# The last chunk's q, k and output turned by DMA, and a plan made anew, in a fused linear-attention and feed-forward kernel

## The chip, the cores and the metric

The kernel runs on one core of a Trainium2 chip. The metric is the device time of one execution in microseconds (us). A core has five engines with queues of their own: TensorE (PE in the profile; its weight loads are PEld), VectorE (DVE), ScalarE (ACT), GpSimd (POOL) and SyncE (SP, which here issues all DMAs). Each engine takes its instructions strictly in order, and waits on semaphores for what the others make.

## The reference

Two layers, one after the other. The first is a gated linear attention: for 4 batches and 8 heads, over 768 positions with a head size of 48, a 48 x 48 state decays by a gate f and takes up the outer product of k and v; the output is q times the state. The second layer takes the result as 3072 tokens of 384 features, through w_in (384 x 2048), the function h cos(h), and w_out (2048 x 384).

```python
f = 1.0 / (1.0 + np.exp(-f_logit))
for t in range(S):
    state = f[:, :, t, :, None] * state + np.einsum('bhd,bhe->bhde', k[:, :, t], v[:, :, t])
    y[:, :, t] = np.einsum('bhd,bhde->bhe', q[:, :, t], state)
...
x = attn_out.transpose(0, 2, 1, 3).reshape(B * S, H * D)
h = x @ w_in
return (h * np.cos(h)) @ w_out
```

## The kernel before

**Chunks.** The 768 positions of a batch are cut into 6 chunks of 128, so there are 24 chunks, numbered 0 to 23. `decay` (line 515) makes the running decay of two chunks at a time: the load of f_logit, Exp and Ln on ACT, a cumulative sum as matmuls on PE (op "cum"), and two Exp on ACT that give `b` and `bi` (line 578). Chunks 0 to 11 go in interleaved pairs through `attend2` (line 633), chunks 12 to 23 singly through `attend` (line 795).

**One chunk in `attend`.** POOL multiplies q by `b` and k by `bi` into the bf16 tile `qk` (op "qk", line 800). `qk` has to be turned, so that the head features lie on partitions. There are two ways. Either PE makes eight transposes into PSUM (op "tr", line 818) and DVE or ACT copies them out (op "qkt"); or, for chunks in `TURN_QK`, SP issues one DMA transpose from `qk` to the tile `qkt` (op "tq", line 809). Then PE makes the scores (line 831), DVE masks them into `am` (line 835), PE updates the state (op "ps", line 845; DVE and POOL scale it, lines 596 and 603), and PE makes y from the state and from `am` (lines 859 and 863). `finish` (line 612) copies y to the bf16 tile `yb` and turns it into a part of `xT`, again in one of two ways: three PE transposes (op "trx", line 626) and a copy (op "xe"), or, for chunks in `TURN_Y`, one DMA transpose from `yb` to `xT` (op "ty", line 618). All the plain copies of these helpers carry line 513.

**Units.** `moe` (line 894) takes two units of 128 tokens (chunks 0 and 1) and eleven of 256 (two chunks each). For a unit of 256, PE makes h in four blocks of 12 matmuls (line 907), ACT takes the cosine (line 915), DVE multiplies into `gT` (line 924), and PE makes the output, 16 matmuls for each chunk (line 934). It is copied to `ot`, and SP stores it (line 942). The first h of a unit waits for the whole `xT` of its chunks. The weights come in four pieces of w_in and four of w_out: a DMA each (line 479) into a staging tile, and a cast to bf16 on POOL, DVE or ACT (op "wc", line 485).

**Buffers that matter here.** `qk` four, `qkt` three, `ld` fourteen halves, `yb` two, `ot` four, the staging tiles and `gT` together six; of PSUM, three pairs of banks for h.

**The order.** It is not the order of the code. Every operation is first recorded by `Plan.op` (line 132) with its inputs, its outputs, a cost for each engine that could run it, and a priority. `Plan.run` (line 161) then lays out the whole program: it picks again and again, among the operations that could start within 120 ns of the earliest, the one of lowest priority number, gives it to the engine on which it would end first, and at last sorts everything by the planned start. So the program is a static order for each engine, PE's and SP's too. The numbers that steer it are tables:

- `PR` has a priority for each kind of operation and chunk, unit, group or piece: "f", "k", "q", "v" for the loads, "at" for the work of a chunk, "tq" and "ty" for the DMA transposes, "h" and "o" for the units, "w_in" and "w_out" for the loads of the weights, "wc" for their casts.
- `PR["gate"]` says, for each of the six groups of four chunks, after which cosine its first exponential may come. ACT has one function table for Exp and Ln and another for the cosine and loads a table at each change.
- `PIN` ties operations, by their number in the record, to one engine. Numbers 1, 3, 5 and 7 are the casts of the w_in pieces 0 to 3, and 9, 11, 13 and 15 those of w_out.
- `BLOCK`, `LEAD` and `FETCH` belong to `fetched` (line 167), which counts PE's instructions: a block of 256 is asked for when the one before it is entered, and if it is entered less than `FETCH` ns after it was asked for, the planned cost of that operation grows by the rest. With `FETCH` at 0 it never grows.
- In the first 36 us the plan also fills idle time of PE with matmuls on zeros (`keep_warm`, line 443, shown as line 448).

Of the kernel before, what the change touches and what calls it, by code (L numbers as in the profile page):

```python
# [116 lines left out]
class Plan:  # L117
# [4 lines left out]
    FORM = 96.0  # L122
    WARM = 1000.0, 36000.0
    SPARE = 300.0
    BLOCK, LEAD, FETCH = 256, 187, 0.0
    TABLE = 1290.0
    WINDOW = 120.0

# [3 lines left out]
    def op(self, name, eng, fn, reads=(), writes=(), prio=0.0, table=None, lat=0.0, grp=None,  # L132
           dma=None, form=("full", "full"), count=0):
        o = Op()
        if PIN.get(len(self.ops)) in eng:
            eng = {PIN[len(self.ops)]: eng[PIN[len(self.ops)]]}
        o.name, o.eng, o.fn, o.prio, o.table = name, eng, fn, prio, table
# [149 lines left out]
def apart(tc, o, base):  # L287
# [13 lines left out]
    if banks and len(others) == len(banks):  # L301
        for b in banks:
# [7 lines left out]
FREE_GROUPS = 1  # L310
HALVED = [0, 2]
COLUMNS = [0]
TURN_Y = range(14, 23)
TURN_QK = range(10, 23)
PR = {
    "at": [-27.91, -77.01, -56.28, -9.17, -0.94, -73.7, -81.2, 39.48, -37.57, -208.65, -211.06, -60.08,
          -83.16, -243.89, -50.42, -56.25, 1.3, -2.3, 29.67, 79.95, 98.34, -55.29, 97.21, 135.16],
    "dec": [17.99, -244.81, 110.38, -107.76, -115.06, -57.64],
    "f": [-126.5, 9.16, -68.42, 63.89, -29.77, -28.09, -25.9, -101.11, -12.97, -46.6, -13.01, -73.8, 5.03,
          -19.04, 46.31, -11.98, 36.02, -5.88, 14.64, -12.03, -9.82, 91.12, 135.61, 80.29],  # L320
    "h": [71.32, -87, -76.49, -17.17, 21.33, -10.88, 23.01, -55.39, -81.13, -168.15, 42.49, -185.2, -65.32],
    "k": [-86.38, -44.94, -46.44, -77.89, -10.71, -14.47, -10.3, 16.65, 19.58, 33.88, 24.75, -42.47, 93.38,
          56.3, 64.2, 82, 99.55, 66.33, 75.6, 103.33, 149.48, 152.06, 180.76, 236.21],
    "o": [-48.11, -58.72, 67.27, 96.81, 129.67, 114.46, -1.43, 88.44, -1.17, 210.3, 20.96, 63.38, 132.01],
    "q": [-102.19, 18.13, -43.75, -58.53, -20.96, -20.69, 3.65, 30.77, 13.57, 38.94, 22.63, -27.69, 43.05,
          64.32, 73.74, 93.93, 83.65, 126.33, 120.02, 148.55, 160.95, 173.59, 319.64, 340.67],
    "tq": [48.59, 92.1, 81.02, -144.86, -187.26, -106.78, -170.82, 10.27, -66.65, -84.42, -111.64, -134.39,
          -84.57, 73.12, -78.38, -82.54, -126.4, -224.07, -57.89, 90.43, 53.23, 51.1, 158.93, 99.76],
    "ty": [88.78, 44.77, 51.02, -49.47, -165.27, -158.37, -101.69, 50.45, 31.53, -89.25, 92.4, -10.66,
          -109.03, 30.59, -136.55, -158.16, -176.89, -143.38, -109.75, -9.6, -42.19, -39.15, -87.93, -26.78],  # L330
    "v": [-46.79, 17.23, -41.07, 7.71, -23.55, -71.11, 10.76, 43.67, 2.59, -102.67, 11.36, 155.56, 68.43,
          17.25, 83.31, 55.29, 17.8, 46.36, 78.93, 34.36, 62.06, 117.69, 104.33, 11.01],
    "w_in": [-39.88, -40.08, -39.64, -38.03],
    "w_out": [-34.2, -33.96, -37.04, -33.75],
    "wc": [-70.63, -33.41, 50, 25.03, -16.34, 18.34, -16.44, -221.86],
    "gate": [None, 2, 4, 12, 20, 24],
}
PIN = {1: "DVE", 7: "POOL", 9: "DVE", 11: "POOL", 13: "POOL", 15: "POOL", 34: "POOL", 35: "DVE", 36: "DVE", 37:
       "ACT", 39: "ACT", 43: "DVE", 55: "DVE", 82: "DVE", 101: "DVE", 103: "POOL", 104: "POOL", 105: "POOL",
       111: "ACT", 122: "ACT", 124: "DVE", 125: "DVE", 127: "ACT", 148: "DVE", 154: "ACT", 166: "DVE", 167:  # L340
       "DVE", 170: "ACT", 172: "ACT", 184: "ACT", 186: "ACT", 187: "DVE", 189: "ACT", 210: "ACT", 216: "ACT",
       228: "POOL", 229: "DVE", 230: "DVE", 231: "POOL", 232: "POOL", 234: "DVE", 238: "DVE", 248: "ACT", 250:
       "DVE", 251: "DVE", 274: "ACT", 280: "DVE", 292: "POOL", 294: "POOL", 295: "POOL", 296: "POOL", 302:
       "ACT", 315: "DVE", 316: "DVE", 318: "DVE", 357: "DVE", 360: "DVE", 361: "POOL", 373: "DVE", 399: "ACT",
       436: "POOL", 445: "ACT", 468: "DVE", 489: "ACT", 498: "DVE", 505: "POOL", 514: "DVE", 536: "DVE", 542:
       "ACT", 566: "ACT", 578: "DVE", 600: "ACT", 621: "ACT", 629: "ACT", 636: "POOL", 667: "DVE", 673: "ACT",
       688: "ACT", 697: "DVE", 704: "ACT", 735: "ACT", 741: "DVE", 756: "ACT", 765: "DVE", 774: "DVE", 778:
       "DVE", 801: "DVE", 813: "ACT"}


def build(nc, cpool, ppool, q, k, v, f_logit, moe_w_in, moe_w_out, out):
# [260 lines left out]
    def finish(n, y, ycut, prio):  # L612
# [3 lines left out]
             reads=[y], writes=[yb], prio=prio)  # L616
        if n in TURN_Y:
            P.op("ty", {"SP": 420.0}, lambda e: nc.sync.dma_start_transpose(out=x.ap, in_=yb.ap),
# [14 lines left out]
    def attend2(b, c, n, ld, bt, bi, prio):  # L633
# [6 lines left out]
        for i in range(2):  # L640
# [8 lines left out]
            reads=[vf], writes=[vb], prio=prio)  # L649
        turned = n in TURN_QK  # L650
        twin = lambda j, p, e: qkv()[:, j, e, 2 * p:2 * p + 2, :].rearrange("p h d -> p (h d)")
# [143 lines left out]
    def attend(b, c, n, ld, bt, bi, i, prio):  # L795
# [11 lines left out]
        pair = lambda j, p: qkv()[:, j, 2 * p:2 * p + 2, :].rearrange("p h d -> p (h d)")  # L807
        if n in TURN_QK:
            P.op("tq", {"SP": 420.0}, lambda e: nc.sync.dma_start_transpose(out=qkt.ap, in_=qk.ap),
# [235 lines left out]
```

## Time and profile before

| what | value |
|---|---|
| five runs, median (lowest to highest) | 187.97 us (187.48 to 188.49) |
| the profiled execution, its own time | 186.72 us |
| its span, from the first to the last instruction | 184.9 us |
| mean granted TensorE clock | 0.998 of full |
| DVE product for gT, line 924 | 60.1 us in 48 instructions |
| ACT cosine, line 915 | 53.5 us in 48 instructions |
| matmuls of h, line 907 | 68.0 us in 624 instructions |
| matmuls of the output, line 934 | 68.9 us in 400 instructions |
| ACT table loads | 10, of 1283 ns each |
| bytes moved | 34.51 MB |

The profile is one execution as the hardware profiler saw it. "Busy" of an engine leaves out its waits. Matmuls overlap, and their ends are modelled: a group's mean duration is longer than what one of them adds to the time, which is read from the times at which they start or from the chain of waits. That chain is followed back from the last instruction, at each step to what released it or to the instruction before it on its engine. Times within it count from the span's start.

### The profile page before, as it was taken

How to read it: one execution, taken by the hardware profiler on the slowest of the kernel's cores; microseconds unless marked ns; L12 is line 12 of the kernel's file. 1: busy time of each engine (PE TensorE's matmuls, PEld its weight loads, DVE VectorE, ACT ScalarE, POOL GpSimd, SP SyncE). 2: the span in 40 equal slices, each digit the busy share in tenths (PEclk: the TensorE clock that was granted, in tenths of full speed). 3: DMA queues.
4: the chain of work that ended last, by engine and by line, in shares of the span. 5: the costliest groups of instructions: out<-in, count | busy, mean ns of one | idle time of the engine just before them, and what ended most of it. 6: DMA issues, size and time to landing. Idle time of an engine off the chain costs nothing.

```text
span 184.9 us, 5205 instructions
## 1 busy us (share of the span) xinstructions
PE 178.3 (96%) x2169; PEld 130.4 (71%) x2169; DVE 130.9 (71%) x168; ACT 124.7 (67%) x156; POOL 69.6 (38%) x103
## 2 busy tenths in 40 slices
PE   6999889999999999999999999999999999999993
PEld 2556678767788775777776677876677876788663
DVE  5488978937779998358697568793579892577520
ACT  5684378997897699964789878699665820646401
POOL 8308473323726663531416734812681230000000
PEclk9999999999999999999999999999999999999999
DMA  5999999999999999798999989996965013111022
GB/s 140 276 260 342 375 379 349 247 270 294 247 207 211 252 171 216 157 235 171 205 202 232 137 206 197 216 214 127 238 136 113 29 25 85 43 46 43 12 77 85
DMA packets 99783, 34.51 MB, mean 187 GB/s; under 512 B 92976, under 2 KB 98224, under 8 KB 99760
## 3 DMA queue, kind: packets, MB, share of 16 engines
q1 hardware_dynamic: 99760, 34.19, 80.0%
q8 instruction: 17, 0.28, 0.7%
q14 instruction: 6, 0.05, 0.1%
HBM read 25.17 MB, written 4.72 MB: 162 GB/s over the span
## 4 chain that ended last, share of the span: by engine, by line
PE 83%; SPq 7%; DMA 5%; POOL 1%; DVE 1%; issue 1%; ACT 0%; POOLq 0%
PE ps L934 35%; PE ps L907 33%; DMA gT<-in_moe_w_in_dram 5%; SPq L499 5%; PE ps L831 2%; SPq L479 2%; PE ps L677 1%; PE ps L693 1%; PE ps L863 1%; PE ps L569 1%; PE ps L626 1%; PE ps L743 1%; PE ps L845 1%; PE ps L859 1%; PE ps L711 1%; POOL w_in_bf L485 1%
## 5 line engine op out<-in xcount | busy, mean ns | idle before, releaser
L924 DVE TENSOR_TENSOR gT<-ps,cosh 128x1024 bf16<-128x1024 f32 x48 | 60.1, 1264 | 16.3 <-ACT cosh L915 15.4
L907 PE MATMUL ps<-xT,w_in_bf 128*128 128x256 bf16 (+1 forms) x624 | 68.0, 264 | 1.0 <-DVE xT L513 0.4
L934 PE MATMUL ps<-w_out_bf,gT 128*128 128x384 bf16 (+2 forms) x400 | 68.9, 320 | 0.0
L915 ACT ACTIVATE cosh<-ps,halfpi 128x1024 bf16<-128x1024 f32 x48 | 53.5, 1114 | 20.6 <-PE ps L907 20.1
L907 PEld LDWEIGHTS <-w_in_bf 128*128 128x128 bf16 x624 | 56.1, 98 | 9.6 <-issue 1.0
L934 PEld LDWEIGHTS <-gT 128*128 128x128 bf16 x400 | 36.2, 98 | 20.3
L603 POOL TENSOR_TENSOR sz<-st,b 64x192 bf16<-64x192 f32 x32 | 16.8, 524 | 26.9 <-DVE st L596 25.8
L513 ACT COPY ot<-ps 128x384 f32<-128x384 f32 (+2 forms) x14 | 6.4, 455 | 20.1 <-PE ps L934 17.3
L800 POOL TENSOR_TENSOR qk<-ld,b 128x384 bf16<-128x384 f32 x12 | 12.0, 1002 | 18.3 <-DMA ld<-in_q_dram 6.6
L835 DVE TENSOR_TENSOR am<-ps,umask 128x1024 bf16<-128x1024 f32 x12 | 14.5, 1217 | 3.7 <-PE ps L831 3.3
L698 DVE TENSOR_TENSOR am<-ps,pmask 128x1024 bf16<-128x1024 f32 x12 | 14.2, 1218 | 2.1 <-PE ps L693 1.6
L800 POOL TENSOR_TENSOR qk<-ld,bi 128x384 bf16<-128x384 f32 x12 | 12.0, 1003 | 6.8 <-DMA ld<-in_k_dram 6.8
L513 DVE COPY ot<-ps 128x384 f32<-128x384 f32 x11 | 6.1, 553 | 11.1 <-PE ps L934 11.1
L537 ACT ACTIVATE f<-f 128x768 f32<-128x768 f32 (+1 forms) x14 | 10.3, 747 | 2.8 <-DMA f<-in_f_logit_dram 2.8
L578 ACT ACTIVATE b<-ps 128x776 f32<-128x776 f32 (+1 forms) x14 | 10.1, 724 | 2.3 <-PE ps L566 1.9
L448 PE MATMUL ps<-zeros 128*128 128x512 bf16 x34 | 10.7, 440 | 1.0 <-DVE halfpi L375 1.0
L549 ACT ACTIVATE sp<-f 128x768 bf16<-128x768 f32 (+1 forms) x14 | 10.4, 751 | 0.3
L513 DVE CAST yb<-ps 128x384 bf16<-128x384 f32 x13 | 7.0, 553 | 4.7 <-PE ps L743 1.9
L642 POOL TENSOR_TENSOR qk<-ld,b 128x384 bf16<-128x384 f32 x6 | 6.0, 1006 | 11.5 <-ACT b L578 11.2
L578 ACT ACTIVATE bi<-ps 128x768 f32<-128x768 f32 (+1 forms) x14 | 10.1, 722 | 0.0
L485 POOL CAST vb<-ld 128x384 bf16<-128x384 f32 (+1 forms) x9 | 6.2, 684 | 9.0 <-PE ps L743 3.7
L596 DVE TENSOR_TENSOR st<-ps,sz 128x384 f32<-128x384 f32 x16 | 8.8, 551 | 0.8 <-PE ps L845 0.7
(82 smaller groups left out, 177.9 us busy)
## 6 DMA issues: line engine op xcount, KB each, us to landing
out_dram<-ot SPq DMA_DIRECT2D x23, 192.0 KB, 2.9
f<-in_f_logit_dram SPq DMA_DIRECT2D x16, 192.0 KB, 4.6
ld<-in_q_dram SPq DMA_DIRECT2D x16, 192.0 KB, 4.2
ld<-in_k_dram SPq DMA_DIRECT2D x16, 192.0 KB, 4.0
gT<-in_moe_w_in_dram SPq DMA_DIRECT2D x4, 768.0 KB, 8.7
gT<-in_moe_w_out_dram SPq DMA_DIRECT2D x4, 768.0 KB, 11.8
ld<-in_v_dram SPq DMA_DIRECT2D x6, 384.0 KB, 5.9
ld<-in_v_dram SPq DMA_DIRECT2D x12, 192.0 KB, 3.6
```

Of the source, the lines that this page charges most:

```text
L448: nc.tensor.matmul(o, lhsT=zeros, rhs=zeros[:, None, :].broadcast_to([128, w // 128, 128]), start=True, stop=True)
L513: (nc.scalar.copy if e == "ACT" else nc.vector.tensor_copy)(out=o, in_=i_)
L549: nc.scalar.activation(out=o, in_=i_, func=AF.Ln, bias=1.0)
L578: nc.scalar.activation(out=out_.ap[:, s, :], in_=pc.ap.rearrange("p (m n) -> p m n", m=w)[:, :, 0:n], func=AF.Exp, scale=sign)
L603: eng().tensor_mul(out=like(S_out.ap, pv())[s, ..., r, :], in0=srcap()[s, ..., r, :], in1=d[..., None].broadcast_to(list(d.shape) + [D]))
L698: P.op("am", {"DVE": dve(1024)}, lambda e, sc=sc, am=am: nc.vector.tensor_mul(out=am.ap.rearrange("p r a n -> p (r a n)").rearrange("p (a ...
L800: P.op("qk", {"POOL": 1020.0}, lambda e, j=j, src=src, dec=dec: E(e).tensor_mul(out=qkv()[:, j, :, 0:D], in0=HB(src.ap), in1=HB(dec.ap[:, ...
L835: P.op("am", {"DVE": dve(1024)}, lambda e: nc.vector.tensor_mul(out=am.ap.rearrange("p r a n -> p (r a) n"), in0=sc.ap.rearrange("p (a n) ...
L907: nc.tensor.matmul(ph.ap[:, g * T:(g + 1) * T], lhsT=w_in_bf[:, f0 // 512, m, f0 % 512:f0 % 512 + 128], rhs=x[:, m, :], start=(g % (G // 2 ...
L915: nc.scalar.activation(out=co.ap, in_=ph.ap, func=AF.Sin, bias=halfpi),
L924: nc.vector.tensor_mul(out=o, in0=i0, in1=i1)
L934: nc.tensor.matmul(po.ap[:, 0:z - a], lhsT=gT.ap[:, j, i * C:(i + 1) * C], rhs=w_out_bf[:, j, a:z], start=(j == 0), stop=(j == KF - 1))
```

## The change

Three things. The ranges `TURN_Y` and `TURN_QK` end one chunk later, so chunk 23 takes the branches of lines 809 and 618 in place of those of lines 812 to 822 and 621 to 629. `FETCH` goes from 0 to 6000 ns. And every table that steers the plan is new: all priorities, the gates of five groups, and the pins. No function changes.

```diff
-    BLOCK, LEAD, FETCH = 256, 187, 0.0
+    BLOCK, LEAD, FETCH = 256, 187, 6000.0
...
-TURN_Y = range(14, 23)
-TURN_QK = range(10, 23)
+TURN_Y = range(14, 24)
+TURN_QK = range(10, 24)
 PR = {
...
-    "f": [-126.5, 9.16, -68.42, 63.89, -29.77, -28.09, -25.9, -101.11, -12.97, -46.6, -13.01, -73.8, 5.03,
...
+    "f": [-156.28, -27.46, -102.33, 55.49, -51.41, -10.97, -49.32, -124.08, -16.08, -95.15, -9, -54.92, 6.66,
...
-    "h": [71.32, -87, -76.49, -17.17, 21.33, -10.88, 23.01, -55.39, -81.13, -168.15, 42.49, -185.2, -65.32],
+    "h": [89.12, -76.25, -84.41, -8.25, 26.05, -6.24, -60.38, -155.86, -100.59, -152.98, -1.62, -225.53,
+          -49.38],
...
-    "o": [-48.11, -58.72, 67.27, 96.81, 129.67, 114.46, -1.43, 88.44, -1.17, 210.3, 20.96, 63.38, 132.01],
+    "o": [-69.04, -74.3, 64.43, 127.49, 122.04, 120.51, 4.64, 193.56, 93.37, 263.81, 109.22, 166.42, 273.51],
...
-    "w_in": [-39.88, -40.08, -39.64, -38.03],
-    "w_out": [-34.2, -33.96, -37.04, -33.75],
-    "wc": [-70.63, -33.41, 50, 25.03, -16.34, 18.34, -16.44, -221.86],
-    "gate": [None, 2, 4, 12, 20, 24],
+    "w_in": [-70.01, -67.62, -59.98, -62.34],
+    "w_out": [-56.29, -58.38, -51.79, -58.25],
+    "wc": [-32.08, 88.38, 156.71, 81.9, 22.29, 161.89, 159.33, -51.89],
+    "gate": [None, 4, 6, 4, 17, 27],
 }
-PIN = {1: "DVE", 7: "POOL", 9: "DVE", 11: "POOL", 13: "POOL", 15: "POOL", 34: "POOL", 35: "DVE", 36: "DVE", 37:
...
+PIN = {7: "POOL", 9: "POOL", 13: "DVE", 33: "POOL", 34: "DVE", 35: "DVE", 43: "DVE", 82: "DVE", 101: "POOL",
...
```

The tables "at", "dec", "k", "q", "tq", "ty" and "v" change in the same way, entry by entry.

## The prediction

> **What bounds the kernel now.** I read the page first, for the engines' shares and the slices.
>
> ```profile
> span 184.9 us, 5205 instructions
> ...
> PE 178.3 (96%) x2169; PEld 130.4 (71%) x2169; DVE 130.9 (71%) x168; ACT 124.7 (67%) x156; POOL 69.6 (38%) x103
> ...
> DMA  5999999999999999798999989996965013111022
> ```
>
> TensorE (PE) is busy for 96% of the span, the others for 71% or less. The DMA engines are nearly full for three quarters of the span and nearly idle in the last quarter. Matmul ends are modelled, so I don't take the 96% at its word: the chain of waits, in order of time, says whether PE really sets the end.
>
> ```profile
> 14.41 10.12 DMA gT<-in_moe_w_in_dram
> 24.57 0.08 issue
> 24.65 1.48 POOL w_in_bf L485
> 26.18 7.57 PE ps L907 x84
> ...
> 59.78 0.71 DVE xT L513 x2
> ...
> 87.31 0.49 ACT yb L513
> 87.83 0.57 DVE yb L513
> ...
> 148.70 0.45 PE ps L818 x8
> ...
> 164.84 0.17 PE ps L626 x3
> ...
> 171.54 10.45 PE ps L934 x80
> 182.02 0.27 ACT ot L513
> ```
>
> Columns are start, length, what. Three stages show. To 26.18 us the chain runs through transfers: the last piece of w_in lands at 24.5 us and is cast. From 26.18 to 182.0 us it is PE from end to end, with two short exceptions at 59.8 and 87.3 us. From 182.0 to 184.9 us it is the last copy and store. So PE's own work in the middle 155.8 us is what a saving must come from, or the time at which that stretch begins, or the few waits inside it. A microsecond saved on DVE, ACT or POOL counts only there.
>
> **What the change removes.** For chunk 23 the eight transposes of line 818 and the three of line 626 go. The chain prices them start to start: 0.45 + 0.17 = 0.62 us, that is 56 ns each. The same matmuls have a duration of 219 ns in their groups, but they overlap, and only the start-to-start price is on the path. Gone too are one eviction of qkt (0.68 us on DVE, at 152.3 us) and one of xT (0.36 us on DVE, at 165.0 us); these lie beside PE's work and I count them as nothing, since the chain touches neither. If PE waited for DVE there, as it did at 59.8 us, they would be worth their length.
>
> The Trainium skill, "TensorE: Matmul & The Clock Gate", section "Part 4: PE-mode transpose", gives about 275 ns for one such transpose inside a kernel. By that the eleven would be worth 3.0 us in place of 0.62 us; the measured 56 ns from start to start speaks against counting it so.
>
> **What it adds.** Two DMA transposes on SP's queue.
>
> ```profile
> q8 instruction: 17, 0.28, 0.7%
> ...
> qkt<-qk SPq DMA_TRANSPOSE x13, 3.7
> xT<-yb SPq DMA_TRANSPOSE x9, 3.0
> ```
>
> One of each kind is added: 3.7 us (range in the trace 3.0 to 4.7) and 3.0 us (2.3 to 4.1) from issue to landing, with 1.29 and 1.21 us of SP's queue.
>
> The turn of q and k: chunk 23's product qk ends on POOL at 139.46 us (the last row of line 800), and its scores (line 831) run on PE at 159.38 us. The three qkt buffers are held by chunks 20 to 22; the first is let go by line 859 at about 146.4 us. Issued then, the turned tile lands by 146.4 + 4.7 = 151.1 us, 8 us ahead of its use. Covered: 0.
>
> The turn of the output: yb of chunk 23 is done at 163.53 us, xT today at 165.40 us. By DMA it is 163.6 + 3.0 = 166.6 us, 1.2 us later (2.3 us at the slowest landing, 0.5 us at the quickest). Behind it is the last unit's h (line 907, 48 matmuls at 109 ns, 5.2 us), queued on PE, and behind that its cosine, product and o. What hides it is o of earlier units: the final run of 80 matmuls of line 934 lasts 10.45 us, and only 32 of them (32 x 162 ns = 5.2 us) belong to the last unit, so 5.2 us can go ahead of h. After h, cosine and product end 2.4 us later (171.54 to 173.96 us), while the last unit's own o now begins at about 176.8 us, a margin of 2.8 us. An h that is 1.2 us later still leaves 1.6 us. I take 0; without any reordering it would cost 1.2 us, which is the upper end. On SP's queue the wait for yb stands ahead of stores; there are four ot buffers and PE makes one tile in 16 x 162 ns = 2.6 us, so a store late by 2 us holds up nobody.
>
> **The new order.** All priorities, most pins of engines and five gates change, and the plan now holds a block of 256 PE instructions back until 6 us after the one before it was asked for. Does PE wait for its instructions today? Queue q8 brings 17 blocks. PE's waits name none: those called "issue" after 26 us, on the side of the weight loads, sum to 4.3 us in pieces of at most 0.6 us, most of them at changes of tile shape (line 831, eight times). The table by stage gives the pace:
>
> ```profile
> 10.00:21.00 11.00, 10.13 (x227) 6.14 (x225) 9.95 (x15) 5.50 (x11) 4.71 (x7) 1.00 1.10 317
> ...
> 140.00:160.00 20.00, 20.00 (x208) 14.97 (x207) 13.55 (x17) 8.46 (x10) 3.01 (x6) 1.00 0.25 64
> ```
>
> The densest stage has 227 matmuls in 11 us; a block is 128 matmuls with their weight loads, so 6.2 us (6.3 us from 21 to 26 us, by 101 in 5 us). From 26 us on a block lasts 9 us or more. Even if a block truly took 6 us to arrive, the trace offers nothing to win: I take 0 for this part.
>
> The Trainium skill, "Runtime: NRT & Kernel Launch", section "Instruction fetch mechanics", says that the cost of crossing such a block is mostly hidden. It speaks against a gain from the new constant: by it the part is 0, while by the constant every microsecond by which a block is run in less than 6 us would be lost; no wait in this trace stands for such a loss.
>
> What a new order can move is bounded by the rows. First, the start. The last w_in piece is cast on POOL:
>
> ```profile
> L485 DVE CAST w_in_bf<-gT 128x1536 bf16<-128x1536 f32 x3 | 2.9, 953 | 0.4 <-DMA gT<-in_moe_w_in_dram 0.4
> ...
> L485 POOL CAST w_in_bf<-gT 128x1536 bf16<-128x1536 f32 x1 | 1.5, 1468 | 0.7 <-DMA gT<-in_moe_w_in_dram 0.7
> ```
>
> With the new priorities the pieces go out as 0, 1, 3, 2 in place of 1, 0, 2, 3, and only piece 3, no longer the last, stays pinned to POOL. The last one may then go to DVE: 1468 - 953 = 0.5 us gained, as PE stands waiting for it. At the other end piece 3, third to land at 22.6 us, waits on POOL behind a pair of sz (22.17 to 23.2 us) and is there at 24.8 in place of 23.6 us, which if PE has nothing else costs up to 1.2 us. What the first four chunks load is nearly in the order of before (v of chunk 0 one step later), so the 14.4 us of transfers ahead stay. I take 0.3 us gained, nearer to the row of the DVE cast. Second, the waits inside PE's stretch: 0.6 us at 59.9 us (from the last transpose's 56 ns to line 907 at 60.54 us) and 0.4 us at 88.0 us (the timeline's idle time of PEld before line 626), together 1.0 us, are all that a better order could close; a worse one could open as many again. I take 0.
>
> **The sum.** -0.62 - 0.3 = -0.92 us. The profiled execution took 186.72 us, 184.9 us of span and 1.8 us around it: after, 185.8 us. The runs shown have a median of 187.97 us, 1.25 us above that execution; the same step from there gives **187.05 us**, said as 187.0.
>
> **Rivals.**
>
> (a) The new order also closes the waits: -0.62 - 0.5 - 1.0 = -2.1 us, **185.9 us**. For it: those waits are for xT and yb of the very kind that a planner moves, and PE has o to put in. Against it: an order that removes one wait on a static queue usually makes another.
>
> (b) The gain is taken back: the start or the turned output costs what the transposes save. With the 1.2 us of late xT uncovered, or the third w_in piece late by as much, -0.62 + 0.6 to 1.2 is 0 to +0.6 us, **about 188.2 us**. It is also the case in which the plan's new constant, having nothing to remove, only shifts work. For it: 0.62 us is small against everything that is reshuffled. Against it: the 5.2 us of o at the end and the 8 us of slack ahead of the scores.
>
> (c) Slower: ACT's exponentials come ahead of the cosines that PE needs. Group 3's gate moves from the 12th cosine to the 4th. Today ACT has loaded the table of exponentials at 34.92 us, does groups 1 and 2, and returns to cosines at 53.58 us; meanwhile PE lives on o of the first three units and the attention of chunks 4 to 7. If group 3 is done in that same stretch, its two decays add, by their groups, 2 x (0.84 + 0.84 + 0.82 + 0.82) = 6.6 us of ACT before the next cosine. PE can run ahead by the three pairs of ph banks alone, 36 matmuls x 109 ns = 3.9 us. What is left, 2.7 us, is PE idle: -0.92 + 2.7 = +1.8 us, **189.8 us**. It decides once the delay of the first cosine after the exponentials passes the 3.9 us of cover. For it: the gate allows it, and ACT is 19.8 of 24 us busy between 26 and 50 us. Against it: two table loads less (2 x 1.28 us), and attention of more chunks becomes ready as filler.
>
> **How the numbers follow.** The forecast gets 0.44, (a) 0.13, (b) 0.18, (c) 0.25. A measurement tells 0.3% (0.56 us) from no change, so faster means under 187.4 and slower over 188.5 us. Forecast and (a) are faster, 0.57; (b) is the same, 0.18; (c) is slower, 0.25. The forecast's own range is 186.2 to 187.4 us. The range over the cases goes from 185.4 us, half a microsecond below (a) since those waits are rounded and others of 0.1 to 0.3 us stand in PE's list, to 189.7 us, which leaves out about half of (c): some 0.15 to 0.2 outside.
>
> **What would show it.** Right: 2158 matmuls in place of 2169; 14 and 10 DMA transposes; no row of line 818; line 626 with 36; the chain of waits PE alone from about 26 us to 181.4 us, the final run of line 934 shorter than 80 or ended 0.6 us sooner; scores of chunk 23 without a wait for a DMA. For the start: the last w_in cast on DVE, and 128-column h finished earlier than today. Wrong: PE idle before line 907 for an xT that comes by DMA in the last 20 us (b), or PE idle in 45 to 75 us with the cosine of line 915 just ahead of it (c); or PE waits for "issue" of a microsecond and more, which would say that instructions do arrive late. A stretch of PE that begins after 27 us would make the forecast wrong by itself.

## The result, and the profile after

| | before | after |
|---|---|---|
| median of all runs | 187.09 us (79 runs, 186.28 to 189.12) | 186.54 us (44 runs, 185.60 to 187.95) |
| ratio, 95% interval | | 0.9966 (0.9953 to 0.9979) |
| profiled execution, span | 184.9 us | 184.2 us |

The kernel is 0.34% faster: 0.64 us of 187.09 us, with an interval of 0.39 to 0.88 us. The ratios are of mean times, without executions more than 1.5% above the fastest of their kernel; the medians in the table are 0.55 us apart. The five runs shown ahead of the prediction had a median 0.9 us above that of the 79, so the absolute forecast of 187.0 us lies 0.5 us above the measured median although the step itself was forecast as 0.92 us, more than was measured. From the median of the 79 the same step would have given 186.2 us, 0.4 us too low. Lines of the changed kernel that stand behind its tables have moved by two: h is now line 909, the output 936, `ty` 620, `tq` 811.

First the engines on the page of the changed kernel (busy time, share, instructions):

```profile
span 184.2 us, 5172 instructions
...
PE 176.6 (96%) x2160; PEld 130.0 (71%) x2160; DVE 127.0 (69%) x162; ACT 121.1 (66%) x153; POOL 75.2 (41%) x110
...
DMA  5999999999997999897998894997779083310012
```

PE is as full as before. It has 9 matmuls fewer, which is 11 transposes gone and 2 more fillers on zeros (36 for 34). DVE and ACT have 3.9 and 3.6 us less, and POOL 5.6 us more: 2.7 us of it are five more casts of v, and 1.5 us one more cast of w_in. What these shifts are worth in the time isn't shown.

The chain of waits in order of time (start, length, what), at the start, in the middle and at the end:

```profile
23.88 1.98 PE ps L909 x24
25.86 1.29 PE ps L450 x6
27.16 6.70 PE ps L909 x84
33.86 4.55 PE ps L936 x28
...
48.84 3.21 POOL qk L644 x3
52.10 0.62 PE ps L679 x8
...
153.52 0.55 PE ps L833 x16
...
156.87 3.25 PE ps L936 x20
160.12 10.48 PE ps L909 x96
170.61 10.45 PE ps L936 x80
181.08 0.27 ACT ot L515
```

At the start, the 84 matmuls that began at 26.18 us begin at 27.16 us, behind six fillers. In both kernels 60 matmuls of h run ahead of these 84. In the changed kernel twelve of the 60 are of the wide form (109 ns each, against 55 ns), so fewer wide ones are left and the 84 take 6.70 us in place of 7.57 us. The first matmul of the output starts at 33.86 us in place of 33.75 us: in this profile the start has lost 0.1 us. In the middle the chain leaves PE for long stretches, at 48.8 us for instance, where POOL's products are what PE's transposes of line 679 wait for. At the end PE is unbroken: the scores of chunks 22 and 23 run together at 153.5 us, 20 matmuls of the output come ahead of h, then h of the last two units in one piece (96 matmuls), then 80 of the output. From the first matmul of the output to the last copy it is 181.08 - 33.86 = 147.2 us, against 182.02 - 33.75 = 148.3 us before: 1.05 us less, of which 0.62 us are the transposes. Behind the last copy the span has 0.2 us more than before.

The DMA view has the fourteenth and the tenth transpose. Their median landings are 3.9 us (3.7 us before) and 2.6 us (3.0 us before):

```profile
q8 instruction: 17, 0.28, 0.7%
...
qkt<-qk SPq DMA_TRANSPOSE x14, 3.9
xT<-yb SPq DMA_TRANSPOSE x10, 2.6
```

PE's own waits between 26 and 182 us, on the matmul side, are one line where the kernel before had three:

```profile
PE ps L679 <- POOL qk L644: 0.4, 1, 0.4
```

### The profile page after: what moved, and what is told of

The parts are those of the page before. It is cut to its first block, busy times and chain, and to the rows that moved or that the text cites. A ratio compares the mean times of both kernels' runs of the same rounds, so it can differ in the third digit from the quotient of the medians.

```text
span 184.2 us, 5172 instructions
## 1 busy us (share of the span) xinstructions
PE 176.6 (96%) x2160; PEld 130.0 (71%) x2160; DVE 127.0 (69%) x162; ACT 121.1 (66%) x153; POOL 75.2 (41%) x110
## 4 chain that ended last, share of the span: by engine, by line
PE 70%; POOL 11%; DMA 5%; SPq 4%; DVE 4%; issue 2%; ACT 0%; POOLq 0%
PE ps L909 29%; PE ps L936 28%; POOL qk L802 5%; SPq L501 3%; DMA ld<-in_v_dram 3%; POOL sz L605 3%; POOL qk L644 2%; DVE am L700 2%; DMA ld<-in_q_dram 2%; PE ps L679 1%; DVE qkt L515 1%; PE ps L833 1%; PE ps L450 1%; SPq L811 1%; PE ps L695 1%
## 5 line engine op out<-in xcount | busy, mean ns | idle before, releaser
L909 PE MATMUL ps<-xT,w_in_bf 128*128 128x256 bf16 (+1 forms) x624 | 67.0, 264 | 0.0
L515 ACT COPY ot<-ps 128x384 f32<-128x384 f32 (+1 forms) x15 | 7.0, 468 | 20.1 <-PE ps L936 19.9
L802 POOL TENSOR_TENSOR qk<-ld,b 128x384 bf16<-128x384 f32 x12 | 12.0, 1000 | 16.2 <-DMA ld<-in_q_dram 11.7
L487 POOL CAST vb<-ld 128x384 bf16<-128x384 f32 (+1 forms) x14 | 8.9, 646 | 21.6 <-DMA ld<-in_v_dram 10.2
L515 DVE COPY ot<-ps 128x384 f32<-128x384 f32 (+1 forms) x10 | 5.4, 541 | 10.6 <-PE ps L936 10.6
L515 ACT CAST yb<-ps 128x384 bf16<-128x384 f32 x15 | 7.0, 479 | 8.1 <-PE ps L865 4.4
L644 POOL TENSOR_TENSOR qk<-ld,b 128x384 bf16<-128x384 f32 x7 | 7.3, 1054 | 7.8 <-DMA ld<-in_q_dram 6.0
```

The lines of the kernel that those rows point to most:

```text
L515: (nc.scalar.copy if e == "ACT" else nc.vector.tensor_copy)(out=o, in_=i_)
L644: P.op("qk", {"POOL": 1050.0, "DVE": 750.0}, lambda e, j=j, i=i, src=src, dec=dec: E(e).tensor_mul(out=parts[j][i].ap.rearrange("p e h d - ...
L802: P.op("qk", {"POOL": 1020.0}, lambda e, j=j, src=src, dec=dec: E(e).tensor_mul(out=qkv()[:, j, :, 0:D], in0=HB(src.ap), in1=HB(dec.ap[:, ...
L909: nc.tensor.matmul(ph.ap[:, g * T:(g + 1) * T], lhsT=w_in_bf[:, f0 // 512, m, f0 % 512:f0 % 512 + 128], rhs=x[:, m, :], start=(g % (G // 2 ...
```

## Experiments

All ratios are to the kernel before, run beside it on the same chip.

**1. The new order with chunk 23 on TensorE.** Is the gain the transposes or the order?

```diff
 # in the changed kernel
-TURN_Y = range(14, 24)
-TURN_QK = range(10, 24)
+TURN_Y = range(14, 23)
+TURN_QK = range(10, 23)
-... 765: "ACT", 777: "ACT", 799: "DVE", 805: "DVE", 811: "ACT"}
+... 765: "ACT", 778: "ACT", 801: "DVE", 807: "DVE", 813: "ACT"}
```

> The changed kernel with chunk 23 turned by TensorE again (ranges end at 23, the pins of the operations recorded behind it shifted to stay with their operations); all other tables new. Theory (the gain is the eleven transposes at 56 ns each): 0.62 us of the 0.64 us are given back, so within 0.1% of the kernel before, and the chain of TensorE ends some 0.6 us later than in the changed kernel. Rival (the new order is the gain, the turned chunk is hidden anyway): still 0.3% to 0.4% faster than before.

Measured: 1.001 (0.9981 to 1.0039), 187.73 us. It was run once more, beside the changed kernel:

> The changed kernel with chunk 23 turned by TensorE, measured once more to narrow the interval. Theory (the transposes are the gain): between 0.9985 and 1.0025 of the kernel before, 0.3 to 0.5% behind the changed kernel of the same call. Rival (the order is the gain): level with the changed kernel.

> The changed kernel itself beside the two others: 0.9953 to 0.9979 of the kernel before by the measured interval; it is here so that the kernel with the transposes on TensorE stands against it on the same chip.

Measured: 0.9977 (0.9945 to 1.0009), 187.58 us, beside 0.9956 (0.9931 to 0.9982), 186.58 us. Without the DMA turns the new order alone lies at 1.001 and 0.9977, so no gain can be told from none; with them it lies at 0.9956 to 0.9966 in three measurements. The 0.9977 is a little outside the 0.9985 to 1.0025 that was expected of the theory, and 0.2% behind the changed kernel where 0.3 to 0.5% were expected, so by the ratios alone it stands between the theory and its rival. The direct comparison on that chip is sharper: the runs have a mean of 187.42 us with the transposes on TensorE and 186.71 us with the DMA turns, 0.7 us apart (0.2 to 1.2 us by resampling the runs). And the first profile shows where the eleven stand on PE's chain:

```profile
145.52 0.45 PE ps L820 x8
...
157.98 0.30 PE ps L628 x3
```

That is 0.75 us in this order. The gain is in the turns, as far as these intervals reach; that the order adds a few tenths can't be excluded.

**2. The turn without the new order.** First with the old tables, from which the plan is laid out anew:

```diff
 # in the kernel before
-TURN_Y = range(14, 23)
-TURN_QK = range(10, 23)
+TURN_Y = range(14, 24)
+TURN_QK = range(10, 24)
-... 765: "DVE", 774: "DVE", 778: "DVE", 801: "DVE", 813: "ACT"}
+... 765: "DVE", 777: "DVE", 799: "DVE", 811: "ACT"}
```

> The kernel before with only the two ranges extended, so that chunk 23 is turned by DMA, and the same priorities and gates (pins shifted to stay with their operations); the plan is laid out anew from the old tables. Theory (the turn alone is worth 0.62 us where the order leaves it hidden): between 0.6 us faster and, since the old tables put chunk 23's DMA transpose ahead of those of chunks 20 to 22 on the queue, up to 3 us slower; a wait of TensorE for xT or qkt after 140 us would show the second. Rival (the turn needs no new tables): 0.6 us faster, ratio 0.9967.

Measured: 1.0076 (1.0045 to 1.0106), 188.52 us: slower by 1.4 us although PE has 0.6 us less to do. The chain of waits shows where:

```profile
156.47 0.21 PE ps L863 x8
...
159.45 0.56 DVE yb L513
160.02 2.28 DMA xT<-yb
162.31 0.05 issue
162.35 10.71 PE ps L907 x96
```

The y that PE ends at 156.68 us is another chunk's, and is copied at once. The timeline has PE's next y from 158.5 to 159.0 us, after a mask on DVE. Its copy yb begins at 159.45 us, behind the following mask, and then the transfer's 2.3 us are waited for. PE's list names 1.7 us for `xT<-yb` where the kernel before had none. PE makes one more y and from 160.7 us has nothing to run until the transfer lands.

Then with the old order kept on every engine, only the turning itself replaced where it stands:

```diff
 # in the kernel before
-                for j in range(2):
+                for j in range(2 if n < 23 else 0):
...
-            P.op("qkt", {...}, lambda e: cp(e, qkt.ap, ...), ...)
+            P.op("qkt", {...}, lambda e: cp(e, qkt.ap, ...) if n < 23 else
+                nc.sync.dma_start_transpose(out=qkt.ap, in_=qk.ap), ...)
...
-            for m in range(KM):
+            for m in range(KM if n < 23 else 0):
...
-        P.op("xe", {...}, lambda e: cp(e, x.ap, pxv()), ...)
+        P.op("xe", {...}, lambda e: cp(e, x.ap, pxv()) if n < 23 else
+             nc.sync.dma_start_transpose(out=x.ap, in_=yb.ap), ...)
...
-            apart(tc, o, P.banks)
+            if o.seq not in (773, 774, 779, 780):
+                apart(tc, o, P.banks)
```

The last lines drop what the kernel declares of these four operations' PSUM banks (`apart`): turned by DMA, they no longer use them.

> The kernel before in its own order on every engine; only the eleven transposes of chunk 23 are left out and its two copies out of PSUM become DMA transposes at the same place of the program. Theory of the prediction: 0.62 us less on TensorE, and at the end, with no o moved ahead, h waits some 1.0 to 1.2 us for the xT that lands later, so 0.4 to 0.6 us slower than before (ratio 1.002 to 1.003), with a wait of TensorE for the DMA of xT at about 165.5 us and none for qkt. Rival (the later landing is hidden even so): 0.6 us faster, 0.9967.

Measured: 1.0034 (1.0001 to 1.0066), 188.05 us, 0.6 us slower. The chain of waits at the end:

```profile
163.61 0.57 DVE yb L513
164.18 0.02 issue
164.19 2.33 DMA xT<-yb
166.52 0.05 issue
166.57 1.48 PE ps L909 x12
```

h waits for the xT of chunk 23, which lands 2.33 us after its issue. The four matmuls of the output that stand between cover the first part; PE idles 0.6 us at 165.8 us. A second wait had not been expected: 0.6 us at 156.6 us, again for an xT (an earlier chunk's, 2.35 us in flight). Chunk 23's other transpose now stands ahead of it on SP's queue, from 153.50 to 154.75 us, so it goes out at 154.84 us where it went out at 153.23 us in the kernel before. A third, of 0.3 us at 142 us, comes before either of chunk 23's transposes is issued, so it isn't theirs. Either half of the change by itself is no gain.

**3. The price of a transpose on TensorE.** Eighty more of them where chunk 23 has its eight.

```diff
 # in the kernel before
-                for j in range(2):
+                for j in list(range(2)) * (11 if n == 23 else 1):
```

> The kernel before with the eight TensorE transposes of chunk 23 issued eleven times over, into the same bank, so 80 more of them, in one run. Priced start to start (56 ns each) they cost 4.4 to 4.5 us: about 191.9 us beside a kernel before of 187.4. Priced by the duration of their group (219 ns) they would cost 17.5 us, and by the 275 ns of the Trainium skill, "TensorE: Matmul & The Clock Gate", section "Part 4: PE-mode transpose", 22 us. Rival (TensorE has room at 148 us, and its work there is hidden): 0.

Measured, in two runs: 1.0224 (1.0164 to 1.0285), 191.81 us, that is 4.2 us (3.1 to 5.3) or 53 ns each. The chain has them as one row:

```profile
149.10 4.92 PE ps L818 x88
154.02 0.17 PE ps L845 x4
```

4.92 us / 88 = 56 ns. The group's duration of 219 ns and the 275 ns of the Trainium skill ("TensorE: Matmul & The Clock Gate", section "Part 4: PE-mode transpose") are not what one costs in a row of them on a busy PE; here the measurement decides. Nor is PE's work at 148 us hidden.

**4. The start: are the late fillers in the way?** The changed kernel runs six matmuls on zeros at 25.7 to 27.0 us, when all casts of w_in are done.

```diff
 # in the changed kernel
-            if o in P.warm:
+            if o in P.warm and P.warm[o][0] < 24000.0:
```

> The changed kernel without the last stretch of filler matmuls on zeros (six of 216 ns, at 25.7 to 27.0 us of its profile), its order otherwise the same. Theory (TensorE sets the end from 20 us on, and all four w_in pieces are cast by 25.6 us, so the fillers stand ahead of real work): 1.0 to 1.3 us faster than the changed kernel, so 0.9% faster than before (ratio 0.990 to 0.992). Rival (what comes next is bound by the loads of chunks 4 to 7 and the attention chain at 43 to 52 us, so an earlier start is lost there): no faster than the changed kernel (0.9966).

Measured: 0.9979 (0.9947 to 1.001), 186.91 us: no faster than the changed kernel. The theory falls. The timeline (start, length, engine, line, operation, idle before and what ended it) names what PE was really waiting for:

```profile
22.88 1.28 ACT L917 ACT_TABLE_LOAD   x1
...
24.17 1.42 DVE L487 CAST w_in_bf<-gT 128x1536 bf16<-128x1536 f32 x1
24.18 3.12 ACT L917 ACTIVATE cosh<-ps,halfpi 128x1024 bf16<-128x1024 f32 x3
25.50 3.69 DVE L926 TENSOR_TENSOR gT<-ps,cosh 128x1024 bf16<-128x1024 f32 x3
26.84 1.36 PE L909 MATMUL ps<-xT,w_in_bf 128*128 128x256 bf16 x11 [1.01 <-DVE gT L926]
```

With the fillers gone PE idles in their place, 1.0 us, until DVE's first product has let go of a pair of PSUM banks. Two things stand ahead of that product. One is the cast of the last w_in piece on DVE, 1.42 us long: the product begins at 25.50 us, as the cast ends. The other is its cosine, which begins behind ACT's table load and ends at 25.29 us. Without the cast the product could have begun some 0.2 us sooner and no more, so most of the wait is the cosine's. In the kernel before, the table load and the cosine came 0.75 us earlier:

```profile
22.13 1.28 ACT L915 ACT_TABLE_LOAD   x1
23.43 1.11 ACT L915 ACTIVATE cosh<-ps,halfpi 128x1024 bf16<-128x1024 f32 x1
```

In both kernels the table load begins when ACT's copy of a yb ends, and the new order puts 24 matmuls of h ahead of the y that this copy waits for. The fillers only stood where PE had to wait.

**5. Are the gate and the fetch constant at work at all?** With the gate of group 3 at the 12th cosine, or with `FETCH` at 0, the changed kernel's planned order is the same on every engine, and so are its fillers. There was nothing to run. In the kernel before, `FETCH` at 6000 changes the length of one stretch of fillers and no order. It may still have steered the search for the tables; that wasn't tried.

**6. A wait that comes and goes.** The profile of the changed kernel in experiment 1 had PE waiting for an xT at 139 us, by 0.5 us; the one first shown had not. On SP's queue the DMA transpose of that xT stands behind the load of chunk 22's q.

```diff
 # in the changed kernel
         order = P.run()
+        at = {o.seq: o for o in order}
+        order.remove(at[752])
+        order.insert(order.index(at[646]) + 1, at[752])
```

> The changed kernel with one step moved on SyncE's queue: the load of chunk 22's q goes out behind, not ahead of, the DMA transpose for which h at 139 us waits. Theory (the run-to-run wait of 0.2 to 1.1 us for that xT comes from what stands and flies ahead of it on the queue): issue 0.6 us earlier, the wait of TensorE at 139 us shrinks to under 0.3 us, and the kernel is 0.2 to 0.6 us faster than the changed one, ratio 0.993 to 0.996 to the kernel before. Rival (the wait only moves on, since the chain behind it waits elsewhere): level with the changed kernel.

> The changed kernel once more beside it, for a comparison on the same chip: 0.9953 to 0.9979 of the kernel before, and a wait for xT at 139 us of 0.1 to 1 us in its profile.

Measured: 0.9939 (0.991 to 0.9968), 186.45 us, beside 0.9959 (0.9925 to 0.9993), 186.49 us. The chain of waits of the changed kernel in that run:

```profile
133.74 0.57 SPq L493
134.31 0.05 issue
134.36 0.02 SPq L620
134.38 0.03 issue
134.41 4.71 DMA xT<-yb
139.11 0.05 issue
139.16 2.79 PE ps L909 x24
```

And with the load moved behind:

```profile
133.96 3.17 PE ps L909 x29
137.13 0.33 PE ps L833 x8
137.46 4.08 PE ps L909 x36
```

The load's issue (0.57 us) and 4.71 us of flight led to PE's h; with the order swapped the chain stays on PE and the wait is gone. The transpose goes out 0.65 us sooner, at 133.76 us, and lands at 136.07 us: its flight has shrunk from 4.71 to 2.31 us, so half of the flight came with the load ahead of it. In the time it can't be told: the ratio is better by 0.2%, the intervals overlap, and the medians differ by 0.04 us. It is at best a little faster than both kernels.

## Why the prediction was right

**The direction, and the largest term.** The eleven transposes at 56 ns start to start, 0.62 us, are the term that came as said: experiment 3 confirms the price, and experiment 1 loses the gain when they go back to PE. The sum was -0.92 us and the measured step is -0.64 us (0.39 to 0.88 us). That this is nearly the one term is partly luck: in the first profile the start lost 0.1 us, the waits inside gave 0.4 us and the end lost 0.2 us. And the absolute range of 186.2 to 187.4 us was set from a median 0.9 us too high: from there the measured step would have given 187.3 us, near its upper end.

**The cover of the two DMA turns.** Right for the new order. The last transposed q and k was issued at 146.6 us, as forecast when line 859 (now 861) lets a buffer go, and its scores ran at 153.5 us; it landed at 151.2 us, so the margin was 2.3 us and not 8, since the new order has the scores earlier. The last transposed y was issued at 157.7 us and landed at 160.0 us. Ahead of the last unit's h PE had 20 matmuls of the output (3.3 us), as the step asked, and then h of the unit before (48 x 109 ns = 5.2 us), which the step had not named; it waited for nothing. The step put the cost without such cover at up to 1.2 us. Experiment 2 shows 0.6 us of waiting at the end in the old order in place, and 1.7 us with the old tables laid out anew. In place there was another 0.6 us at 156.6 us, which the prediction, looking at chunk 23's own path, had not priced: a DMA transpose added to SP's queue also delays its neighbours, there by 1.6 us.

Two readings in the working were off without harm. The last unit's output is 48 matmuls, of 384, 256 and 128 columns, and not 32 of 384; its 5.2 us are right. And the pair of sz ahead of the cast on POOL ended at 23.94 us in the profile before, not at 23.2 us. In the changed kernel it ended at 23.27 us, so the cast was done at 24.80 us, as said, by luck.

**The fetch constant.** Costed at 0, and it is 0: the order is the same without it. PE's waits called "issue" stay at 0.3 us at most.

**The start was the step that failed.** It was put at 0.3 us gained, since the last w_in piece would go to the faster DVE. It did go to DVE, and was there at 25.6 us in place of 26.1 us. But the start lost 0.1 us in the first profile, and 0.3 and 1.1 us in the two others of the changed kernel, all against the one profile before. The estimate took the cast as what PE stands waiting for. Experiment 4 shows that PE then waited for PSUM banks, held until DVE's first product, which came at 25.53 us in place of 24.57 us: its cosine was 0.8 us later behind ACT's table load, and the cast held it for 0.2 us more. The cast itself also took 1.27 us where the row quoted had 0.95 us. Two of the prediction's own signs went against it here: the 84 matmuls begin after 27 us, at 27.16 us, and the last 128-column matmul of h starts at 33.6 us, not earlier than the 33.5 us of before. PE begins h at 20.0 us, 1.6 us earlier than before, so the later wait costs the start little on the whole.

**The waits inside PE's stretch.** Put at 0 net, between 1.0 us closed and as many opened. The two of before are gone (0.6 us at 59.9, 0.4 us at 88 us) and others stand in their place: 0.6 us at 51.4 us, for POOL's product of q, about 0.25 us at 121.2 us, and up to 0.5 us at 139 us in the changed kernel's three profiles. The middle of the first profile is 1.05 us shorter, 0.4 us more than the transposes; in the second and third, where the wait for xT is 0.5 and 0.4 us, it is 0.8 and 0.7 us shorter. The sign of a chain on PE alone from 26 us on did not come: the chain leaves PE at 43 and at 98 us, though PE itself waits there for 0.6 and 0.3 us at most. So forecast (a), that the new order closes the waits as well, was answered the way that spoke against it.

**Rivals (b) and (c).** (b), the gain taken back, did not come in the new order; experiment 2 has its mechanism in the old one. (c), exponentials ahead of the cosines, was empty: the gate that allows it binds nothing, as the order is the same with the old gate.

The count of 2158 matmuls given as a sign was off by the two fillers that the new plan adds.

## What to carry to other kernels

Where one engine is busy from end to end, an instruction is worth its start-to-start time on that engine, not its duration, and moving it elsewhere gains that much only if the order is remade to cover the longer way: here the move alone lost 0.6 to 1.4 us, the new order alone gained nothing that could be told, both together gained 0.64 us. Before costing a faster cast, ask what the waiting engine will wait for next once the cast is early: here for PSUM banks, and behind them for a cosine and its table load. And a wait seen in one profile and not in the next is a margin; find it in several profiles before trusting either.

## What the runs showed that was not expected

A DMA transpose of the same size takes 2.3 us when the queue is quiet (the last 30 us) and 4.4 to 4.9 us at 134 us, with a load ahead of it: 4.71 us above, and 4.42 and 4.94 us in two other profiles of the new order. With the load behind it, it took 2.31 us there too (experiment 6). Its landing makes PE wait 0.2 to 1.1 us at 139 us in five profiles of the new order. In the changed kernel's first it also flew 4.40 us, and PE did not wait: it landed 0.2 us ahead of its use.

The start varies too: the first h of the changed kernel began at 20.0 us in one profile, 21.0 us in another and 20.3 us in a third, and the first matmul of the output followed by the same amount.
